# One decode step of attention and a bilinear GLU: scores moved to TensorE, P @ V moved to VectorE

## The chip, the cores and the metric

The kernel runs on one NeuronCore of a Trainium2 chip. The metric is the device time of one execution in microseconds (us); lower is better. The core has TensorE (PE in the profile; its weight loads are listed apart as PEld), VectorE (DVE), ScalarE (ACT), GpSimd (POOL) and SyncE (SP), and 16 DMA engines that share every large transfer.

## The reference, cut to what matters

```python
def _A_ref(x, k_cache, v_cache, wq, wo):          # B=2, D=448, H=16, Sk=8192, Dh=256, all f32
    q = (x @ wq).reshape(B, 1, H, Dh).transpose(0, 2, 1, 3)
    scores = jnp.einsum("bhqd,bhkd->bhqk", q, k_cache) * Dh ** -0.5
    p = softmax(scores, axis=-1)
    o = jnp.einsum("bhqk,bhkd->bhqd", p, v_cache)
    return o.transpose(0, 2, 1, 3).reshape(B, 1, H * Dh) @ wo

def _B_ref(x, w_gate, w_up, w_down):              # F=1792
    return ((x @ w_gate) * (x @ w_up)) @ w_down

h  = x + _A_ref(layernorm(x), ...)
h2 = h + _B_ref(layernorm(h), ...)
```

There are two batch rows with one query each. Every one of the 32 pairs of batch row and head reads its own 8 MB of K and 8 MB of V once; the caches are 537 MB of the 561 MB that the kernel reads.

## The kernel before, in words

The program is unrolled; nothing in it branches. It walks through 32 pairs (h, b), head by head, batch row 0 and then 1. Four tiles of 4 MB (32 KB in each of 128 partitions) form a ring with the tag `ring`. Each pair loads K into two of them and then V into the other two (`load_cache`, L146); a partition holds 32 whole keys of 256 numbers. SyncE issues all large loads in the order K, K, V, V, and waits before each until the ring tile that it overwrites has been read for the last time. Before the V loads of every fourth pair stands the load of the next weight tile `w`, which holds wq and wo of two heads (`load_w`, L140, 1792 KB).

Scores are made on VectorE. For each of the 64 keys of a partition, one SCALAR_TENSOR_TENSOR (L203) multiplies 256 numbers of K by the query, which stands in every partition, and its accumulator leaves the sum in a column of `s`. The accumulator is read out by an instruction of its own, DVE_READ_ACCUMULATOR, so a pair takes 128 VectorE instructions for its scores. The maximum over all keys goes DVE (L212), PE (L214), DVE (L216), PE (L218), ACT (L220), and one activation makes `p` (128 x 64, L223).

P @ V runs on TensorE (L234): 32 matmuls with two columns of `p` as the weights and two keys of V (512 numbers) as the moving operand, in four groups of PE columns. Then `o_ps` is copied (L239), transposed (L243), scaled (L249), and after batch row 1 multiplied by wo into `acc_ps` (2 x 448, L252).

After the last pair come the loads of the second half, on the same ring and queue: `wg_t`, `wu_t` (3136 KB each, L262) and `wd_t` in four parts (L271). The residual `h_sb` (L277) is transposed to `T_h`, centred and spread into `xr`; `g_ps` and `u_ps` (L299) are the two projections, `hm` (L323) their product, `hm_ps` and `hmT` its transpose, `y_ps` (L333) the output of w_down. Four small copies and one DMA (L346) write the result. A scheduler orders the instructions that lie between two loads.

Of the kernel before, what the change touches and what calls it, by code (L numbers as in the profile page):

```python
# [8 lines left out]
F32 = mybir.dt.float32  # L9
AF = mybir.ActivationFunctionType  # L10
# [5 lines left out]
P = 128  # L16
HALF = 64
DC = 4
DW = (P, P, P, HALF)
JC = 32  # L20
NCH = SK // (P * JC)
NJ = SK // P
RING = 4
WQ, WO = 3 * 2 * DH + DH, 4 * D
# [3 lines left out]
NF = F // P  # L28

# [8 lines left out]
def tile_decode_block(  # L38
# [3 lines left out]
    k_cache: bass.AP,  # L42
    v_cache: bass.AP,
# [10 lines left out]

# [6 lines left out]
    qpool = ctx.enter_context(tc.tile_pool(name="qpool", bufs=4))  # L61
    work = ctx.enter_context(tc.tile_pool(name="work", bufs=2))
    ps_q = ctx.enter_context(tc.tile_pool(name="ps_q", bufs=2, space=bass.MemoryType.PSUM))
    ps_s = ctx.enter_context(tc.tile_pool(name="ps_s", bufs=2, space=bass.MemoryType.PSUM))
    ps_1 = ctx.enter_context(tc.tile_pool(name="ps_1", bufs=1, space=bass.MemoryType.PSUM))


    x_sb = const.tile([B, DC * P], F32, name="x_sb")
    nc.scalar.dma_start(x_sb[:, :D], x.rearrange("b s d -> (b s) d"))
    nc.scalar.dma_start(x_sb[:, D:], x.rearrange("b s d -> (b s) d")[:, D - HALF :])  # L70
    ident = const.tile([P, P], F32, name="ident")
    make_identity(nc, ident)
    ones = const.tile([P, P], F32, name="ones")
    nc.vector.memset(ones, 1.0)
    avg = const.tile([P, P], F32, name="avg")
    nc.vector.memset(avg, 1.0 / D)
    row = const.tile([1, P], F32, name="row")
    nc.vector.memset(row, DH**-0.5)
    eps_t = const.tile([P, 1], F32, name="eps_t")
    nc.vector.memset(eps_t, EPS)  # L80
    xr = const.tile([P, DC + 1, B, 16], F32, name="xr")
    nc.gpsimd.memset(xr[:, DC - 1 :], 0.0)
    junk = [const.tile([P, DH], F32, name=f"junk{i}") for i in range(4)]

    sel = const.tile([P, 2], F32, name="sel")
    nc.vector.tensor_reduce(
        sel, ident.rearrange("p (g r) -> p r g", r=32)[:, :2, :], axis=AX.X, op=ALU.add
    )  # L90
    o_ps = [ps_1.tile([P, 2 * DH], F32, name=f"o_ps{i}") for i in range(2)]
    for t in o_ps:
        nc.vector.memset(t, 0.0)
    acc_ps = ps_1.tile([B, D], F32, name="acc_ps")
    y_ps = ps_1.tile([P, P], F32, name="y_ps")
# [12 lines left out]
    def center(h, tag):  # L108

        mean = ps_s.tile([P, B], F32, tag="sm", name=f"mean_{tag}")  # L110
# [10 lines left out]
    def spread(dst, src, n):  # L121

        for rows, c, to in LAYOUT:
            k = rows.stop - rows.start
            nc.vector.tensor_copy(
                dst[rows, to], src[rows, c][:, :, :, None].to_broadcast([k, c.stop - c.start, B, n])
            )

    def transposed(src, tag):
        ps = ps_s.tile([P, DC, B], F32, tag="sm", name=f"T_ps_{tag}")  # L130
        for c in range(DC):
            nc.tensor.transpose(ps[:, c, :], src[:, c * P : (c + 1) * P], ident[:B, :B])
        got = const.tile([P, DC, B], F32, name=f"T_{tag}")
        nc.vector.tensor_copy(got, ps)
        return got


    def load_w(hp):
        t = wpool.tile([P, WQ + WO], F32, tag="w", name=f"w_{hp}")
        nc.sync.dma_start(t, wqo[hp])  # L140
        return t

    def load_cache(src, b, h, c, name):
        t = ring.tile([P, JC, DH], F32, tag="ring", name=f"{name}_{h}_{b}_{c}")
        n = P * JC
        nc.sync.dma_start(t, src[b, h, c * n : (c + 1) * n].rearrange("(p j) d -> p j d", p=P))  # L146
        return t

    w_now = load_w(0)

    xT = transposed(x_sb, "x")


    xc = center(xT, "x")
    var = ps_s.tile([P, B], F32, tag="sm", name="var_x")
# [5 lines left out]
    xn = const.tile([P, DC, B], F32, name="xn")  # L161
    nc.vector.tensor_mul(xn, xc, rstd[:, None, :].to_broadcast([P, DC, B]))
    xb = const.tile([P, DC + 1, B, P], F32, name="xb")
    nc.gpsimd.memset(xb[:, DC - 1 :], 0.0)
    spread(xb, xn, P)

    def queries(hp, w):

        got = []
        for b in range(B):  # L170
            ps = ps_q.tile([P, 2 * DH], F32, tag="q", name=f"q_ps_{hp}_{b}")
            for c in range(DC - 1):
                nc.tensor.matmul(  # L173
                    ps, xb[:, c, b, :], w[:, c * 2 * DH : (c + 1) * 2 * DH],
                    start=(c == 0), stop=False,
                )
            for k in range(2):
                nc.tensor.matmul(  # L178
                    ps[:, k * DH : (k + 1) * DH], xb[:, DC - 1 + k, b, :],
                    w[:, 3 * 2 * DH : WQ], start=False, stop=(k == 1),  # L180
                )
            q = qpool.tile([P, 2, DH], F32, tag="q", name=f"q_{hp}_{b}")
            nc.scalar.activation(q.rearrange("p h d -> p (h d)"), ps, AF.Copy)  # L183
            got.append(q)
        return got
# [215 lines left out]
```

## Time and profile before

| | |
|---|---|
| runs | 1345.97, 1348.38, 1349.16 us; median 1348.38 us |
| profiled execution | span of 1345.7 us from the first to the last instruction; no other time of this execution is given, and the median of the runs lies 2.7 us above its span |
| PE busy | 496.5 us (37%), 2892 matmul records |
| DVE busy | 741.2 us (55%), 4232 instructions |
| ACT busy | 60.6 us (5%), 182 instructions |
| read from HBM | 561.19 MB, 417 GB/s over the span |
| DMA queue of the loads | its packets take 98.2% of the time of 16 DMA engines |
| mean granted TensorE clock | 0.656 |

Busy shares are means over the span. Where the profile lists windows, each row gives a stretch of time, the busy time of each engine in it with the number of instructions, the granted clock, the busy share of the 16 DMA engines and the GB/s that they moved. In the timeline, a row gives the start, the duration, the engine, the line and operation, the tiles written and read, and in brackets the idle time before it with what ended that. The queues q8 and q14 are marked `instruction`: they bring the program's own instructions to the engines.

### The profile page before, as it was taken

The page shows a single profiled execution, that of the slowest core. Times are in us where ns is not written, and L with a number is a line of the kernel's source. Part 1 is how long each engine was busy: PE and PEld are TensorE (multiplying, and loading weights), DVE is VectorE, ACT ScalarE, POOL GpSimd, SP SyncE. Part 2 cuts the span into 40 slices and gives each one's busy share as a digit, 9 for nine tenths or more (in the row PEclk, how much of TensorE's full clock was granted, in tenths as well). Part 3 has the DMA queues.
Part 4 walks back from the last instruction along what each step waited for, and adds up shares of the span by engine and source line. Part 5 has one row for each costly group of instructions (what it writes and reads, how often), then busy time and mean ns, then how long its engine had stood idle before and what let it go on. Part 6 is the DMA issues. An engine that isn't in the chain of part 4 may idle for free.

```text
span 1345.7 us, 10677 instructions
## 1 busy us (share of the span) xinstructions
PE 496.5 (37%) x2892; PEld 165.4 (12%) x2892; DVE 741.2 (55%) x4232; ACT 60.6 (5%) x182; POOL 1.2 (0%) x8
## 2 busy tenths in 40 slices
PE   3344223462224532155331533325343342333217
PEld 1111001120001210011100111101011020111003
DVE  5555664446654366653466634566444665445661
ACT  0000000000000000000000000000000000000000
POOL 0000000000000000000000000000000000000000
PEclk8667676675666865668655677656766576766569
DMA  9999999999999999999999999999999999999994
GB/s 405 428 433 430 433 429 430 431 430 433 432 426 433 430 432 432 428 433 430 425 412 417 430 433 408 411 411 430 430 407 412 413 435 426 411 407 414 417 404 189
DMA packets 20520, 561.87 MB, mean 418 GB/s; under 512 B 2280, under 2 KB 2412, under 8 KB 2668
## 3 DMA queue, kind: packets, MB, share of 16 engines
q1 hardware_dynamic: 20452, 561.20, 98.2%
q8 instruction: 22, 0.36, 0.1%
q14 instruction: 38, 0.31, 0.1%
q10 hardware_dynamic: 8, 0.00, 0.0%
HBM read 561.19 MB, written 0.00 MB: 417 GB/s over the span
## 4 chain that ended last, share of the span: by engine, by line
DMA 71%; DVE 27%; PE 1%; issue 1%; DVEq 0%; ACT 0%; SPq 0%
DMA k<-in_A_k_cache_dram 70%; DVE junk L203 27%; DMA wu_t<-in_B_w_up_dram 2%; PE u_ps L299 0%; PE y_ps L333 0%; DVE hm L323 0%; PE hm_ps L326 0%; DVEq L203 0%; DVE y L345 0%; ACT y L343 0%; SPq L140 0%; DVE hmT L328 0%; DVEq L323 0%
## 5 line engine op out<-in xcount | busy, mean ns | idle before, releaser
L203 DVE SCALAR_TENSOR_TENSOR junk<-k,q 128x256 f32<-128x256 f32 x2048 | 710.9, 420 | 483.6 <-DMA k<-in_A_k_cache_dram 483.6
L234 PE MATMUL o_ps<-v,p 128*2 128x512 f32 x2048 | 297.4, 741 | 37.2 <-DMA v<-in_A_v_cache_dram 37.0
L214 PE MATMUL mT<-ident,m 128*1 128x128 f32 x32 | 11.2, 351 | 624.0 <-DVE m L212 624.0
L203 DVE DVE_READ_ACCUMULATOR junk<-k,q 128x1 f32 x2048 | 168.2, 82 | 0.0
L173 PE MATMUL q_ps<-w,xb 128*128 128x512 f32 x96 | 60.7, 783 | 105.9 <-DMA w<-in_wqo_dram 104.5
L234 PEld LDWEIGHTS o_ps<-v,p 128*2 128x2 f32 x2048 | 53.5, 97 | 251.6 <-issue 197.7
L214 PEld LDWEIGHTS mT<-ident,m 128*1 128x1 f32 x32 | 2.6, 81 | 634.0 <-DVE m L212 613.5
L243 PE MATMUL oT_ps<-sel,o_sb 128*128 128x1 f32 x256 | 33.7, 253 | 23.2 <-ACT o_sb L239 23.2
L173 PEld LDWEIGHTS q_ps<-w,xb 128*128 128x128 f32 x96 | 23.6, 256 | 140.6 <-DMA w<-in_wqo_dram 114.7
L227 DVE RECIPROCAL rl<-l_ps 128x1 f32<-128x1 f32 x32 | 5.4, 169 | 62.9 <-PE l_ps L225 62.9
L252 PE MATMUL acc_ps<-w,oT 128*2 128x448 f32 x64 | 35.8, 695 | 5.6 <-ACT oT L249 5.6
L243 PEld LDWEIGHTS oT_ps<-sel,o_sb 128*128 128x128 f32 x256 | 31.0, 191 | 53.1 <-ACT o_sb L239 53.1
L220 ACT ACTIVATE nb<-nb_ps 128x1 f32<-128x1 f32 x32 | 5.5, 171 | 671.2 <-PE nb_ps L218 671.2
L239 ACT ACTIVATE o_sb<-o_ps 128x512 f32<-128x512 f32 x32 | 19.1, 597 | 353.7 <-PE o_ps L234 353.7
L225 PE MATMUL l_ps<-lsum,ones 128*128 128x1 f32 x64 | 17.3, 340 | 24.9 <-ACT p L223 24.9
L218 PE MATMUL nb_ps<-nm,row 1*128 1x1 f32 x64 | 16.7, 328 | 13.4 <-DVE nm L216 13.4
L216 DVE TENSOR_REDUCE nm<-mT 1x1 f32<-1x128 f32 x32 | 8.9, 279 | 20.4 <-PE mT L214 20.4
L183 ACT ACTIVATE q<-q_ps 128x512 f32<-128x512 f32 x16 | 9.6, 597 | 193.5 <-PE q_ps L178 193.5
L225 PEld LDWEIGHTS l_ps<-lsum,ones 128*128 128x128 f32 x64 | 14.6, 283 | 27.6 <-ACT p L223 27.6
L218 PEld LDWEIGHTS nb_ps<-nm,row 1*128 1x128 f32 x64 | 14.5, 280 | 23.1 <-issue 12.4
L178 PE MATMUL q_ps<-w,xb 128*128 128x256 f32 x64 | 16.5, 380 | 0.0
L178 PEld LDWEIGHTS q_ps<-w,xb 128*128 128x128 f32 x64 | 12.5, 195 | 9.5 <-issue 8.6
(74 smaller groups left out, 74.9 us busy)
## 6 DMA issues: line engine op xcount, KB each, us to landing
k<-in_A_k_cache_dram SPq DMA_DIRECT2D x64, 4096.0 KB, 28.6
v<-in_A_v_cache_dram SPq DMA_DIRECT2D x64, 4096.0 KB, 34.7
w<-in_wqo_dram SPq DMA_DIRECT2D x8, 1792.0 KB, 31.5
wg_t<-in_B_w_gate_dram SPq DMA_DIRECT2D x1, 3136.0 KB
wu_t<-in_B_w_up_dram SPq DMA_DIRECT2D x1, 3136.0 KB, 23.9
wd_t<-in_wd_dram SPq DMA_DIRECT2D x1, 1792.0 KB, 19.7
wd_t<-in_wd_dram SPq DMA_DIRECT2D x1, 672.0 KB, 21.0
wd_t<-in_wd_dram SPq DMA_DIRECT2D x1, 448.0 KB, 21.7
```

The lines of the kernel that those rows point to most:

```text
L173: nc.tensor.matmul(ps, xb[:, c, b, :], w[:, c * 2 * DH : (c + 1) * 2 * DH], start=(c == 0), stop=False,)
L178: nc.tensor.matmul(ps[:, k * DH : (k + 1) * DH], xb[:, DC - 1 + k, b, :], w[:, 3 * 2 * DH : WQ], start=False, stop=(k == 1),)
L183: nc.scalar.activation(q.rearrange("p h d -> p (h d)"), ps, AF.Copy)
L203: nc.vector.scalar_tensor_tensor(junk[j % 4], kt[c][:, j, :], 1.0, q_now[b][:, hh, :], op0=ALU.mult, op1=ALU.mult, accum_out=s[:, col : co ...
L214: nc.tensor.transpose(mT, m, ident)
L216: nc.vector.tensor_reduce(nm, mT, axis=AX.X, op=ALU.max, negate=True)
L218: nc.tensor.matmul(nb_ps, row, nm, start=True, stop=True)
L225: nc.tensor.matmul(l_ps, ones, lsum, start=True, stop=True)
L234: nc.tensor.matmul(o[g : g + 2, :], p[:, 2 * t : 2 * t + 2], vt[c][:, j : j + 2, :], start=(t < 4), stop=(t >= NJ // 2 - 4),)
L239: nc.scalar.activation(o_sb, o, AF.Copy)
L243: nc.tensor.matmul(oT_ps[:, c : c + 1], o_sb[:, (2 * k + c) * P : (2 * k + c + 1) * P], sel[:, k : k + 1], start=(k == 0), stop=(k == 1),)
L252: nc.tensor.matmul(acc_ps, oT[:, c, :], w_now[:, WQ + (hh * 2 + c) * D : WQ + (hh * 2 + c + 1) * D], start=(h == 0 and c == 0), stop=(h == ...
```

## The change: scores on TensorE, P @ V on VectorE, the output projection transposed, the last loads in parts

K is packed on the host so that the 256 numbers of a key lie over partitions (two blocks of 128), and the 8192 keys form 4 groups of 2048. A score matmul has a 128 x 32 weight, the query repeated in 32 columns, and 512 keys as the moving operand; four groups fill the four groups of PE columns. So `s` is a PSUM tile of 128 x 2048: 32 equal rows for each key group. V is packed so that a partition holds, for one key group, the 2048 keys of 8 of the 256 numbers. P @ V is then 8 VectorE instructions over 2048 keys, in place in the V tile, each with an accumulator. The packing is a change of layout; the loads of K and V keep their number, order and size (32 KB in each partition).

The query is made as columns (8 small matmuls in each head). `output` turns the sums into a 128 x 2 x 2 tile by four matmuls with `gsum` and multiplies by wo with wo as the weights: 10 matmuls in each head, with 2 columns moving, into a transposed `acc_ps`. It is called after the first half of the next pair's scores. The scheduler is switched off (`manual_schedule`). V of the last pair comes in four loads, `wu_t` in three, the result is written by two DMAs, and x arrives already transposed in one load.

```diff
+    ctx.enter_context(tc.manual_schedule())
...
+    def load_k(b, h):
+        got = []
+        for n in range(2):
+            t = ring.tile([P, 2, G, HK], F32, tag="ring", name=f"k_{h}_{b}_{n}")
+            nc.sync.dma_start(t.rearrange("p c g k -> p (c g k)"), kc[b, h, n])
...
+    xT = const.tile([P, DC, B], F32, name="xT")
+    nc.scalar.dma_start(xT.rearrange("p c b -> p (c b)"), x)
...
+    def scores(s, q, b, kt, n):
+        for j in range(HK // MM):
+            at = n * HK + j * MM
+            for c in range(2):
+                for g in range(G):
+                    nc.tensor.matmul(
+                        s[g * R : (g + 1) * R, at : at + MM],
+                        q[:, c, b, :],
+                        kt[n][:, c, g, j * MM : (j + 1) * MM],
+                        start=(c == 0), stop=(c == 1),
+                    )
+
+    def output(h, w, oacc, lsum):
+        l_ps = ps_m.tile([P, B], F32, tag="sm", name=f"l_ps_{h}")
+        nc.tensor.matmul(l_ps, ones, lsum, start=True, stop=True)
+        rl = work.tile([P, B], F32, tag="rl", name=f"rl_{h}")
+        nc.vector.reciprocal(rl, l_ps)
+        oT_ps = ps_m.tile([P, B, 2], F32, tag="sm", name=f"oT_ps_{h}")
+        for r in range(G):
+            nc.tensor.matmul(
+                oT_ps[r * R : (r + 1) * R], gsum, oacc[:, :, r::G], start=True, stop=True
+            )
+        oT = work.tile([P, B, 2], F32, tag="oT", name=f"oT_{h}")
+        nc.vector.tensor_mul(oT, oT_ps, rl[:, :, None].to_broadcast([P, B, 2]))
+        for m in range(DC + 1):
...
+            for c in range(2):
+                wo = w[:, h % 2, WQ + c * D : WQ + (c + 1) * D]
                 nc.tensor.matmul(
+                    acc_ps[rows, at, :], wo[:, at * P : at * P + rows.stop - rows.start],
+                    oT[:, :, c], start=(h == 0 and m == 0 and c == 0),
...
+    for i in range(NQ):
         h, b = divmod(i, B)
+        kt = load_k(b, h)
+        if h % 2 == 1 and b == 0 and h + 1 < H:
+            w_next = load_w((h + 1) // 2)
+        vt = load_v(b, h, 2 if i == NQ - 1 else 1)
...
-        for c in range(NCH):
-            for j in range(JC):
-                col = c * JC + j
-                nc.vector.scalar_tensor_tensor(
-                    junk[j % 4], kt[c][:, j, :], 1.0, q_now[b][:, hh, :],
-                    op0=ALU.mult, op1=ALU.mult, accum_out=s[:, col : col + 1],
-                )
+        s = ps_s.tile([P, GK], F32, tag="s", name=f"s_{i}")
+        scores(s, q_now, b, kt, 0)
+        if last is not None:
+            output(*last)
+            last = None
+        scores(s, q_now, b, kt, 1)
...
+        for n in range(2):
+            nc.vector.tensor_reduce(
+                m[:, n : n + 1], s[:, n * HK : (n + 1) * HK], axis=AX.X, op=ALU.max
+            )
...
+        p = work.tile([P, GK], F32, tag="p", name=f"p_{i}")
+        nc.scalar.activation(p, s, AF.Exp, bias=nb, scale=1.0, accum_out=lsum[:, b : b + 1])
...
-        for t in range(NJ // 2):
-            c, j = divmod(2 * t, JC)
-            g = 32 * (t % 4)
-            nc.tensor.matmul(
-                o[g : g + 2, :], p[:, 2 * t : 2 * t + 2], vt[c][:, j : j + 2, :],
-                start=(t < 4), stop=(t >= NJ // 2 - 4),
+        for o in range(NO):
+            v = vt[o // (NO // 2)][:, o % (NO // 2), :]
+            nc.vector.scalar_tensor_tensor(
+                v, v, 1.0, p, op0=ALU.mult, op1=ALU.mult, accum_out=oacc[:, b, o : o + 1]
             )
...
+    wg_t = load_ff(wg, "wg_t", ())
+    wu_t = load_ff(wu, "wu_t", (2 * F, 3 * F))
+    wd_t = load_ff(wd, "wd_t", (8 * D, 11 * D, 13 * D))
...
+    output(*last)
+    hT = const.tile([P, DC, B], F32, name="hT")
+    nc.vector.tensor_add(hT, xT, acc_ps)
```

On VectorE, the end of the last pair and what follows it. In these rows `k_1_1` is the second K tile of batch row 1, `m` and `nm` the maximum, `rl` the reciprocal of the sum, `h_sb` the residual. Before, the last of the 64 score instructions stand in front of the maximum:

```order
L203 SCALAR_TENSOR_TENSOR junk_99,s_4369<-k_1_1_4363,q_1_3775 128x256
L203 SCALAR_TENSOR_TENSOR junk_100,s_4369<-k_1_1_4363,q_1_3775 128x256
L212 TENSOR_REDUCE m_4434<-s_4369 128x1
L216 TENSOR_REDUCE nm_4438<-mT_4436 1x1
L227 RECIPROCAL rl_4449<-l_ps_4447 128x1
L277 TENSOR_TENSOR h_sb<-x_sb,acc_ps 2x448
L278 TENSOR_TENSOR h_sb<-x_sb,acc_ps 2x64
L134 COPY T_h<-T_ps_h 128x8
L100 TENSOR_REDUCE sum_h_h<-T_h 128x2
```

Now, with `oacc` for the sums over a V tile and `ff_ps` for the PSUM tile of the second half:

```order
L241 TENSOR_REDUCE m_2657<-s_2623 128x1 x2
L247 TENSOR_REDUCE nm_2662<-mT_2656 1x1
L263 SCALAR_TENSOR_TENSOR v_1_0_2617,oacc_2535<-v_1_0_2617,p_2668 128x2048 x4
L263 SCALAR_TENSOR_TENSOR v_1_1_2620,oacc_2535<-v_1_1_2620,p_2668 128x2048 x4
L286 MEMSET ff_ps 64x128 x2
L287 MEMSET ff_ps 128x112
L197 RECIPROCAL rl_2695<-l_ps_2693 128x2
L204 TENSOR_TENSOR oT_2702<-oT_ps_2697,rl_2695 128x4
L291 TENSOR_TENSOR hT<-xT,acc_ps 128x8
L120 TENSOR_REDUCE sum_h_h<-hT 128x2
```

The long VectorE work moved from in front of the maximum, where it needs K, to behind it, where it needs V and `p`; it is 8 instructions a pair where 64 stood.

On TensorE, the last pair up to the first projection. Before, with `o_ps` for P @ V:

```order
L214 MATMUL mT_4436<-ident,m_4434 1x128
L218 MATMUL nb_ps_4440<-nm_4438,row 128x1
L225 MATMUL l_ps_4447<-lsum_4445,ones 128x1
L234 MATMUL o_ps_104<-v_1_0_4365,p_4444 2x512 x16
L234 MATMUL o_ps_104<-v_1_1_4367,p_4444 2x512 x16
L243 MATMUL oT_ps_4485<-sel,o_sb_4483 128x1 x4
L252 MATMUL acc_ps<-w_3690,oT_4359 2x448 x2
L132 MATMUL T_ps_h<-ident,h_sb 128x2 x4
```

Now, with `s` for the scores:

```order
L185 MATMUL s_2623<-k_1_0_2613,q_2517 32x512 x16
L185 MATMUL s_2623<-k_1_1_2615,q_2517 32x512 x16
L245 MATMUL mT_2656<-ident,m_2657 1x128 x2
L251 MATMUL nb_ps_2664<-nm_2662,row 128x1
L195 MATMUL l_ps_2693<-lsum_2536,ones 128x2
L200 MATMUL oT_ps_2697<-oacc_2535,gsum 32x4 x4
L210 MATMUL acc_ps<-oT_2702,w_2209 128x2 x6
L210 MATMUL acc_ps<-oT_2702,w_2209 64x2 x4
L130 MATMUL mean_h<-sum_h_h,avg 128x2
```

The 32 large matmuls moved from behind the maximum to in front of it. Behind the last V load stand now four small matmuls and ten with wo as their weights, where the second half of P @ V, its transpose and two matmuls stood.

More of the change, by code (lines that the diff above doesn't have):

```diff
@@ L92, in tile_decode_block @@
[L92 to L95, printed above, removed]
+    acc_ps = ps_1.tile([P, DC, B], F32, name="acc_ps")
     def over_chunks(t, tag):
@@ L160, in tile_decode_block @@
     nc.vector.reciprocal(rstd, std)
[L161 to L172, printed above, removed]
+    xn = const.tile([P, DC + 1, B], F32, name="xn")
@@ L285, in tile_decode_block, with project @@
     )
[L287 to L290 removed]
+    def project(ps, w):
         for c in range(DC):
```

314 lines of the change are left out of this document (160 added, 154 removed).

## The prediction, made before the changed kernel ran

> **What bounds the kernel now.** I read the page first, from engines to DMA.
>
> ```profile
> span 1345.7 us, 10677 instructions
> PE 496.5 (37%) x2892; PEld 165.4 (12%) x2892; DVE 741.2 (55%) x4232; ACT 60.6 (5%) x182; POOL 1.2 (0%) x8
> ...
> GB/s 405 428 433 430 433 429 430 431 430 433 432 426 433 430 432 432 428 433 430 425 412 417 430 433 408 411 411 430 430 407 412 413 435 426 411 407 414 417 404 189
> ...
> q1 hardware_dynamic: 20452, 561.20, 98.2%
> q8 instruction: 22, 0.36, 0.1%
> q14 instruction: 38, 0.31, 0.1%
> ...
> k<-in_A_k_cache_dram SPq DMA_DIRECT2D x64, 4096.0 KB, 28.6
> v<-in_A_v_cache_dram SPq DMA_DIRECT2D x64, 4096.0 KB, 34.7
> w<-in_wqo_dram SPq DMA_DIRECT2D x8, 1792.0 KB, 31.5
> ```
>
> No engine is over 55% busy, while the loads keep 16 DMA engines busy 98.2% of the time. The bytes stay as they are, so at first sight neither does the time move. The next view asks how fast the loads run in each stretch (columns: window, us, busy us of each engine, clock, DMA share, GB/s):
>
> ```profile
> 60.00:350.00 290.00, 108.12 (x595) 35.23 (x595) 163.41 (x936) 12.69 (x39) 0.00 (x0) 0.65 1.00 431
> 350.00:640.00 290.00, 106.55 (x591) 35.05 (x591) 161.95 (x928) 12.69 (x39) 0.00 (x0) 0.65 1.00 431
> 660.00:960.00 300.00, 115.65 (x659) 37.64 (x651) 160.22 (x917) 13.54 (x41) 0.00 (x0) 0.67 0.99 421
> 960.00:1300.00 340.00, 112.78 (x652) 35.09 (x652) 196.06 (x1123) 12.96 (x42) 0.00 (x0) 0.62 0.99 417
> 1328.00:1341.00 13.00, 10.26 (x147) 5.21 (x149) 2.56 (x12) 0.69 (x1) 0.00 (x0) 1.00 0.07 27
> ```
>
> The last row is the key: for the last 13 us of loading, 0.07 of the DMA engines work at 27 GB/s, a sixteenth of 431. **One DMA engine is 13 us late**, 15 have finished, and a load has landed only when all 16 have done their part. In the first half all run at 431 GB/s; from 660 us on the mean falls, because a ring tile can't be loaded again before the late engine has filled it, and the 15 wait.
>
> When did it fall behind? The chain of waits shows how far apart K lands (start, us: the K load ends at their sum):
>
> ```profile
> 480.06 28.55 DMA k<-in_A_k_cache_dram
> 519.88 28.54 DMA k<-in_A_k_cache_dram
> 559.70 28.57 DMA k<-in_A_k_cache_dram
> ```
>
> A pair takes 39.82 us, twice alike. Its 16.78 MB at 431 GB/s are 38.93 us. So the late engine loses 0.9 us in every pair. The DMA view of 60 to 640 us (14.5 pairs) says what else it may carry:
>
> ```profile
> q8 instruction: 9, 0.15, 0.1%
> q14 instruction: 17, 0.14, 0.1%
> ```
>
> These bring instructions. On the page, q8 moved 16 KB a fetch, 0.36 MB in all, 62 bytes for each of PE's 5784 records; q14 8 KB a fetch. At 62 bytes, 8 KB are some 130 instructions, and VectorE executes 4232/32 = 132 in a pair: one fetch of q14 in each pair (17 in 14.5 pairs, the rest for ACT, POOL or SP), which is the rhythm of the loss. q8 comes every 64 us and can't make equal pairs. I conclude: VectorE's fetches all go through one DMA engine, and each costs it 0.9 us (itself, and what it disturbs). 33 fetches make 30 us. The other side agrees: 13 us of lateness at the end, and the 15 engines' waiting, 300 x (1 - 421/431) + 340 x (1 - 417/431) = 18 us: 31 us.
>
> **How late V is.** The loads up to the last V are 128 x 4.194 + 8 x 1.835 = 551.5 MB, 1279.7 us at 431 GB/s. The first is issued by 1.13 us; I take 1.5 for its start:
>
> ```profile
> 0.74 0.39 SPq L140 DMA_DIRECT2D w<-in_wqo_dram  x1
> ```
>
> So the last V could land at 1281 us. The tail of the timeline shows that it lands at 1318.4:
>
> ```profile
> 1309.63 0.22 DVE L212 TENSOR_REDUCE m<-s 128x1 f32<-128x64 f32 x1
> ...
> 1311.53 0.35 ACT L223 ACTIVATE p<-s,nb 128x64 f32<-128x64 f32 x1
> ...
> 1312.54 5.46 PE L234 MATMUL o_ps<-v,p 128*2 128x512 f32 x32
> ...
> 1318.38 3.62 PE L234 MATMUL o_ps<-v,p 128*2 128x512 f32 x32 [0.39 <-DMA v<-in_A_v_cache_dram]
> ...
> 1322.71 1.05 PE L243 MATMUL oT_ps<-sel,o_sb 128*128 128x1 f32 x8 [0.72 <-ACT o_sb L239]
> ...
> 1324.12 1.67 PE L252 MATMUL acc_ps<-w,oT 128*2 128x448 f32 x4 [0.35 <-ACT oT L249]
> ...
> 1326.93 0.17 DVE L134 COPY T_h<-T_ps_h 128x8 f32<-128x8 f32 x1 [0.37 <-PE T_ps_h L132]
> ...
> 1328.56 3.63 PE L299 MATMUL g_ps<-wg_t,xr 128*32 128x512 f32 x32 [0.50 <-DVE xr L125]
> ...
> 1333.56 3.63 PE L299 MATMUL u_ps<-wu_t,xr 128*32 128x512 f32 x32 [1.06 <-DMA wu_t<-in_B_w_up_dram]
> ...
> 1339.03 3.23 PE L333 MATMUL y_ps<-wd_t,hmT 128*2 128x128 f32 x112 [0.28 <-DVE hmT L328]
> ...
> 1342.33 0.28 DVE L345 COPY y<-y_ps 2x128 f32<-2x128 f32 x1 [3.36 <-PE y_ps L333]
> ...
> 1343.51 0.32 SPq L346 DMA_DIRECT2D out_dram<-y  x1
> ```
>
> It is 37 us late, 30 of them by VectorE's fetches; 7 remain, for TensorE's fetches and what I can't name. Behind it lies a tail of 1345.7 - 1318.4 = 27.3 us.
>
> **The change, part by part.** *Fetches.* VectorE's program falls from 4232 instructions to about 676: 420 in the new order, and 256 accumulator reads, one for each of the long instructions. That is 5.3 fetches, 4.8 us instead of 30. TensorE's grows: 1593 matmuls of two records each (but the 68 transposes), each with a weight load, are 6236 records against 5784, so 24 fetches of q8 instead of 22. If they spread over the DMA engines, each engine gets one or two; a 16 KB fetch at 27 GB/s is 0.6 us, with the same disturbance (0.9 less the 0.3 us of 8 KB) 1.2: 2 us for an engine. Loss after: 7 us. Bounds: 5 (VectorE's alone) and 12 (all 7 of the unnamed remain). The last V lands at 1.5 + 1279.7 + 7 = 1288 us, **30 us earlier**.
>
> A page of the Trainium skill speaks against this: Runtime: NRT & Kernel Launch, Instruction fetch mechanics, says that instructions are refilled in 16 KiB blocks by a DMA queue of the sequencer's own and that crossing a block is mostly hidden. By it fewer instructions would save nothing, and the time would be the first rival's. The trace agrees for the waiting instruction, and q8's blocks have that size; q14's are half as large, and what the page leaves out is the load whose DMA engine fetches.
>
> *Does the stream stay fed?* Prices first:
>
> ```profile
> 1308.82 0.42 DVE L203 SCALAR_TENSOR_TENSOR junk<-k,q 128x256 f32<-128x256 f32 x1
> ...
> 1309.17 0.42 DVE L203 SCALAR_TENSOR_TENSOR junk<-k,q 128x256 f32<-128x256 f32 x1
> ```
> ```profile
> L239 ACT ACTIVATE o_sb<-o_ps 128x512 f32<-128x512 f32 x32 | 19.1, 597 | 353.7 <-PE o_ps L234 353.7
> L225 PEld LDWEIGHTS l_ps<-lsum,ones 128*128 128x128 f32 x64 | 14.6, 283 | 27.6 <-ACT p L223 27.6
> L220 ACT ACTIVATE nb<-nb_ps 128x1 f32<-128x1 f32 x32 | 5.5, 171 | 671.2 <-PE nb_ps L218 671.2
> L323 DVE TENSOR_TENSOR hm<-u_ps,g_sb 128x512 f32<-128x512 f32 x1 | 0.7, 692 | 4.4 <-PE u_ps L299 4.4
> ```
>
> VectorE starts a 256-wide instruction every 0.35 us. L323 with 512 elements takes 692 - 420 = 272 ns more than one with 256: 1.06 ns an element, so a 2048-wide one takes 0.35 + 1.90 = 2.25 us (at most 8 x 0.35 = 2.8). Eight are 18.0 us, where 64 took 22.1. A score half is 16 matmuls of 512 columns in four groups, the form of L234: 5.5 us after a pause, 3.6 behind other work. Counted from the landing of the second K tile: scores 5.5, maximum over 1024 from PSUM 1.2 (692 ns and 512 more elements), the small steps 1.9 (from 1309.85 to 1311.53 before, and a transpose more), exponential 2.1 (0.83 ns a column by L239 and L220, 2048 columns, and the accumulator). VectorE starts P @ V at 10.7, when the first V tile (9.7) is there, and ends at 28.7. The V tiles are free at 19.7 and 28.7; their next loads begin at four and five loads after K's landing, 39 and 49. K is free 5 us after landing, needed 29 after. So the queue keeps 20 us in hand everywhere. PE's `output` stands between two score halves and waits for VectorE's 28.7; the K tile of the half in front of it lands at 29: nothing waits. In VectorE's order `rl` waits for that PE step, with an idle VectorE behind it. The start (x in one load of tiny pieces, on ACT's queue; fewer query columns) hides behind 43 us of loads issued at once: the first K tile must be free by 43, and was at 29.
>
> ```profile
> 29.07 28.14 DMA k<-in_A_k_cache_dram
> ...
> 1318.06 1.81 SPq L271 DMA_DIRECT2D wd_t<-in_wd_dram  x4
> ```
>
> The start costs nothing unless x is 14 us late. The four extra issues (two for V, two for wu) take SP 0.45 us each by the second row, within its 20 us; I put them at nothing, and at 2 us if that cover were gone.
>
> *The tail, from the last V landing.* VectorE ends its 8 instructions at 28.7 - 19.5 = 9.2 us; halves of V don't help, since VectorE is behind anyway. Then oT_ps 0.9 (1.05 before, with wider weights) and its product 0.2; ten matmuls with wo as weights, 12 loads of 128 columns at 14.6/64 = 0.23 and 8 of half the width: 3.8; `hT` 0.3; from there to g_ps 1.5 as from T_h before: g_ps starts at 15.9, where it was 10.2. It no longer waits 1.1 us for wu behind g_ps, but seven residual matmuls moved there (0.7): u_ps at 20.6 instead of 15.2. From there to y_ps as before, 5.5 and 3.2; one copy instead of four saves 0.9. PE comes to this from 18 us of rest, and its first 16 matmuls may take 5.5 instead of 3.6: I add 0.7, bounds 0 and 2. Tail: 27.3 + 5.4 - 0.9 + 0.7 = 32.5 us, **5 us longer** (bounds 30 and 35). The loads of the second half ended 22.6 us behind V (1341), and y_ps begins at 26 behind it: they are covered.
>
> **Sum.** 1288 + 32.5 = 1320.5 us of span. The median of the runs, 1348.38, is 2.7 us above the profiled span; so 1323 us, 1.9% faster.
>
> **The rivals.** *The late engine stays late* (the slower side): its 0.9 us a pair come from somewhere else, a fixed slowness. Then the last V lands at 1318.4 as before, and the longer tail decides: 1318.4 + 32.5 = 1350.9, with 2.7 us 1354. It decides as soon as the stream gains less than 5 us. For it: I infer which queue does it from the rhythm. Against it: 132 instructions a pair fit one block too well. The Trainium skill knows such a case, DMA: Bandwidth & Descriptors, Latency and other measured facts: DMA engines 7 and 15 are usually slower, which it ascribes, unsure, to descriptor rings of the GpSimd path. Here one engine is late, not two, and no queue of that path carries loads.
>
> *Both fetch queues on the late engine.* Then of 30 us, 22 fetches of q8 have the larger part, by bytes 0.36 MB to 33 x 8 KB = 0.27 MB: 17 us; 24 of them cost 19, VectorE's 5 some 2. The stream gains 9, the tail takes 5: 1342, median 1345, about no change. Against it: the two pairs above are alike although q8 comes only every 64 us.
>
> *A new stall takes part of the gain*: a ring tile that is released late, or one DMA engine that gets three or four of TensorE's fetches. Each us of it is one; 8 to 15 us give 1331 to 1338.
>
> **How the numbers follow.** The forecast has 0.80. Its upper end is 1331: loss 12 and tail 35. Its lower end is 1313: loss 5, tail 30, and a stream at the 433 GB/s of the better slices, since 431 still contains the late engine (551.5 MB take 6 us less). The new stall has 0.09, both queues 0.05, the fixed slowness 0.06. The range 1313 to 1336 takes in the greater part of the new stall and leaves out some 0.15. A change of 0.3%, 4 us, is about what this measurement can tell from none. Faster: 0.89 (the forecast and the new stall), within 0.3%: 0.05, slower: 0.06.
>
> **What would show it.** q14 with about 10 fetches instead of 38 (some six come ahead of the start); 430 GB/s in all windows up to the end of V; no stretch in which a sixteenth of the DMA engines works alone for 13 us; pairs 38.9 to 39.1 us apart; the last V near 1288. For the tail: VectorE's last long instruction 9 us behind the last V, acc_ps about 4 us long, and an end that no DMA decides. If the fetches fall and the pairs still take 39.8 us, my reading of the late engine is wrong.

## The result, and the profile after

The changed kernel takes 1324.25 us (median of 4 runs, 1323.21 to 1324.97) where the kernel before, run beside it, took 1347.18 us: a ratio of 0.983 (95% interval 0.9816 to 0.9844). The profiled execution has a span of 1323.2 us and took 1324.97 us.

From the page of the kernel after, the span, the engines, the GB/s of each slice and the DMA queues:

```profile
span 1323.2 us, 7506 instructions
PE 499.9 (38%) x3114; PEld 200.2 (15%) x3114; DVE 669.7 (51%) x674; ACT 79.3 (6%) x116; POOL 0.8 (0%) x8
...
GB/s 401 428 436 426 435 430 431 427 435 430 428 433 429 433 430 431 428 432 430 432 432 429 432 430 429 429 433 429 429 433 432 429 431 431 429 428 434 433 422 214
...
q1 hardware_dynamic: 21032, 561.20, 98.8%
q8 instruction: 24, 0.39, 0.1%
q14 instruction: 9, 0.07, 0.0%
```

VectorE executes 674 instructions where it executed 4232, and q14 brings 9 blocks instead of 38. TensorE's q8 brings 24 instead of 22. The GB/s row no longer sinks to 404 to 417 in its second half. The windows say the same (us of PE, PEld, DVE, ACT and POOL, then granted clock, DMA share, GB/s; the last two rows are the end of the loads):

```profile
60.00:350.00 290.00, 114.23 (x692) 46.17 (x688) 145.38 (x141) 16.71 (x25) 0.00 (x0) 0.63 1.00 431
...
660.00:960.00 300.00, 121.77 (x709) 45.15 (x709) 148.85 (x145) 16.43 (x24) 0.00 (x0) 0.62 1.00 431
960.00:1260.00 300.00, 107.04 (x671) 44.30 (x675) 164.16 (x159) 18.94 (x28) 0.00 (x0) 0.63 1.00 431
1304.00:1309.50 5.50, 5.50 (x32) 1.85 (x24) 0.39 (x2) 0.00 (x0) 0.00 (x0) 0.54 0.55 222
1309.50:1320.00 10.50, 7.97 (x166) 4.99 (x164) 1.27 (x5) 0.69 (x1) 0.00 (x0) 1.00 0.01 5
```

The DMA engines are full to the end of the walk over the pairs. In the last 5.5 us of loading they still work at half their rate, 0.55 and 222 GB/s, so none of them is left alone for long. The stretch of 13 us with a sixteenth of the bandwidth is gone, and the last load lands 32 us earlier, at 1309.5 instead of 1341. In the chain of waits, K lands at the sums of these rows (start and duration):

```profile
475.11 34.21 DMA k<-in_kc_dram
...
514.77 33.45 DMA k<-in_kc_dram
...
553.48 33.96 DMA k<-in_kc_dram
```

That is 509.32, 548.22 and 587.44: pairs 38.9 and 39.2 us apart, where they were 39.82. The tail of the timeline (start, us, engine, line and operation, tiles; in brackets the idle time before it and what ended that):

```profile
1268.10 5.33 PE L185 MATMUL s<-k,q 128*32 128x512 f32 x32 [4.60 <-DMA k<-in_kc_dram]
...
1273.51 2.35 DVE L241 TENSOR_REDUCE m<-s 128x1 f32<-128x1024 f32 x2 [15.93 <-PE s L185]
...
1277.31 1.97 ACT L255 ACTIVATE p<-s,nb 128x2048 f32<-128x2048 f32 x1
...
1279.40 2.29 DVE L263 SCALAR_TENSOR_TENSOR v<-v,p 128x2048 f32<-128x2048 f32 x1 [2.76 <-ACT p L255]
...
1294.89 2.29 DVE L263 SCALAR_TENSOR_TENSOR v<-v,p 128x2048 f32<-128x2048 f32 x1
...
1298.34 3.25 PE L210 MATMUL acc_ps<-oT,w 128*128 128x2 f32 x20 [0.84 <-DVE oT L204]
...
1303.35 6.47 PE L312 MATMUL ff_ps<-wg_t,xr 128*32 128x512 f32 x32 [0.50 <-DVE xr L295]
...
1311.36 0.40 PE L333 MATMUL ff_ps<-ident,hT 128*2 128x112 f32 x14 [1.23 <-ACT g_sb L326]
1311.55 3.63 PE L312 MATMUL ff_ps<-wu_t,xr 128*32 128x512 f32 x32
...
1317.00 2.87 PE L351 MATMUL ff_ps<-wd_t,hmT 128*2 128x112 f32 x112 [0.28 <-DVE hmT L346]
...
1320.24 1.09 ACTq L361 DMA_DIRECT2D out_dram<-y  x1
```

The last half of the scores starts when K lands, at 1268.10. The maximum, the exponential and eight VectorE instructions follow, and then the small steps up to the output. Two rows are longer than I had thought: the first projection on `wg_t` takes 6.47 us (L312), and the residual matmuls (L333) wait 1.23 us for an ACT instruction.

### The profile page after: what moved, and what is told of

Read it like the earlier page. It is cut to its first block, busy times and chain, and to the rows that moved or that the text cites. A ratio compares the mean times of both kernels' runs of the same rounds, so it can differ in the third digit from the quotient of the medians.

```text
span 1323.2 us, 7506 instructions
## 1 busy us (share of the span) xinstructions
PE 499.9 (38%) x3114; PEld 200.2 (15%) x3114; DVE 669.7 (51%) x674; ACT 79.3 (6%) x116; POOL 0.8 (0%) x8
## 4 chain that ended last, share of the span: by engine, by line
DMA 83%; PE 15%; DVE 2%; issue 0%; ACT 0%; SPq 0%; DVEq 0%; ACTq 0%
DMA k<-in_kc_dram 83%; PE s L185 13%; DVE v L263 1%; PE ff_ps L312 1%; PE acc_ps L210 0%; PE ff_ps L351 0%; DVE m L241 0%; ACT p L255 0%; DVE hm L342 0%; ACT g_sb L326 0%; PE ff_ps L344 0%; PE mean_h L130 0%; DVE nm L247 0%; SPq L80 0%; PE ff_ps L333 0%
## 5 line engine op out<-in xcount | busy, mean ns | idle before, releaser
L263 DVE SCALAR_TENSOR_TENSOR v<-v,p 128x2048 f32<-128x2048 f32 x256 | 569.5, 2287 | 120.1 <-ACT p L255 70.6
L185 PE MATMUL s<-k,q 128*32 128x512 f32 x2048 | 360.7, 869 | 693.8 <-DMA k<-in_kc_dram 693.8
L241 DVE TENSOR_REDUCE m<-s 128x1 f32<-128x1024 f32 x64 | 75.4, 1219 | 403.8 <-PE s L185 403.8
L185 PEld LDWEIGHTS s<-k,q 128*32 128x32 f32 x2048 | 87.0, 152 | 925.9 <-issue 822.6
L255 ACT ACTIVATE p<-s,nb 128x2048 f32<-128x2048 f32 x32 | 62.9, 1967 | 1.2 <-ACT nb L253 0.2
L165 PE MATMUL q_ps<-xn,w 128*128 128x2 f32 x192 | 40.2, 325 | 0.8 <-PE var_x L142 0.8
L165 PEld LDWEIGHTS q_ps<-xn,w 128*128 128x128 f32 x192 | 38.2, 290 | 1.1 <-PE var_x L142 0.9
L210 PE MATMUL acc_ps<-oT,w 128*128 128x2 f32 (+1 forms) x320 | 31.1, 239 | 6.3 <-DVE oT L204 6.3
L210 PEld LDWEIGHTS acc_ps<-oT,w 128*128 128x128 f32 (+1 forms) x320 | 29.5, 179 | 7.9 <-DVE oT L204 7.7
L263 DVE DVE_READ_ACCUMULATOR v<-v,p 128x1 f32 x256 | 20.9, 82 | 0.0
L168 PE MATMUL q_ps<-xn,w 128*128 128x2 f32 x64 | 16.7, 330 | 0.0
L168 PEld LDWEIGHTS q_ps<-xn,w 128*128 128x128 f32 x64 | 15.8, 302 | 0.0
## 6 DMA issues: line engine op xcount, KB each, us to landing
wu_t<-in_B_w_up_dram SPq DMA_DIRECT2D x1, 896.0 KB, 27.9
```

Of the source, the lines that this page charges most:

```text
L165: nc.tensor.matmul(ps[:, c, :], wh[:, at : at + P], xn[:, k, :], start=(k == 0), stop=False)
L168: nc.tensor.matmul(ps[:, c, :], wh[:, 3 * DH : WQ], xn[:, DC - 1 + c, :], start=False, stop=True)
L185: nc.tensor.matmul(s[g * R : (g + 1) * R, at : at + MM], q[:, c, b, :], kt[n][:, c, g, j * MM : (j + 1) * MM], start=(c == 0), stop=(c == 1),)
L210: nc.tensor.matmul(acc_ps[rows, at, :], wo[:, at * P : at * P + rows.stop - rows.start], oT[:, :, c], start=(h == 0 and m == 0 and c == 0) ...
L241: nc.vector.tensor_reduce(m[:, n : n + 1], s[:, n * HK : (n + 1) * HK], axis=AX.X, op=ALU.max)
L255: nc.scalar.activation(p, s, AF.Exp, bias=nb, scale=1.0, accum_out=lsum[:, b : b + 1])
```

## The experiments

My theory: the stream of loads was late because one DMA engine also fetched VectorE's program, and the change won by shortening that program. Rivals: the new order of the loads or the new layout won it; or that engine is simply slow; or the fetches of any engine cost as much.

### The instructions put back

On the kernel after, nothing is changed but for small instructions that do nothing useful: 112 one-column memsets on VectorE in each of 31 pairs, or 56, or 112 on GpSimd, or 28 small matmuls on TensorE.

```diff
+    fill = const.tile([P, 4], F32, name="fill")
...
+        if i < NQ - 1:
+            for z in range(112):
+                nc.vector.memset(fill[:, z % 4 : z % 4 + 1], 0.0)
```

112 on VectorE. Expected:

> The changed kernel with 112 one-column memsets on VectorE in each of 31 pairs, put where VectorE waits for the scores. They take some 7 us of a pair in which VectorE is idle for about 18 us, so they add instructions to fetch (3472 x 62 bytes = 215 KB, 27 blocks of 8 KB) and next to no time of their own. Fetch theory (one DMA engine carries all of VectorE's fetches and loses 0.9 to 1.0 us by each): 24 to 27 us slower, 1348 to 1351 us, and at the end one DMA engine works alone for some 13 us again. Order theory (the gain came from the new layout, the order of the instructions or the earlier release of the K tiles): no change, 1324 us. Slow-engine theory (one DMA engine is slow whatever it fetches): no change either.

56 on VectorE. Expected:

> The same with 56 memsets in a pair: 1736 instructions, 13.6 blocks. Fetch theory: 12 to 13.5 us slower, 1336 to 1338 us, half of the step with 112. Order theory and slow-engine theory: 1324 us. A theory by which VectorE's time and not its fetches counts would give a threshold: nothing here, something with 112.

112 on GpSimd. Expected:

> The 112 memsets in a pair are on GpSimd, which has no other work, instead of VectorE. If each engine's fetches have a DMA engine of their own, as I suppose for the queue q14, GpSimd's 27 blocks make another DMA engine late by 24 to 27 us: 1348 to 1351 us. If q14 spreads fetches of engines other than VectorE, or if it is VectorE's execution that costs: 1324 to 1326 us.

28 on TensorE, without the tile `fill`. Expected:

> 28 one-column f32 matmuls in a pair on TensorE, behind the exponential: 112 records (two matmuls and two weight loads each), 3472 in all as before, 13.6 blocks of 16 KB on queue q8. If q8 spreads its fetches over the 16 DMA engines: 1 to 2 us slower, 1325 to 1326 us. If q8 uses one DMA engine as VectorE's fetches do: 13.6 x 1.2 to 1.6 = 16 to 22 us slower, 1340 to 1346 us.

All four ran beside a kernel before of 1347.74 us. From the page, q14 and one window at the end of the loads of the run with 112 on VectorE, then q14 and the first window with 56, the same with 112 on GpSimd, and q8 with the matmuls:

```profile
q14 instruction: 36, 0.29, 0.1%
...
1320.00:1325.00 5.00, 4.02 (x24) 1.84 (x28) 1.70 (x11) 0.00 (x0) 0.00 (x0) 0.50 0.07 29
```
```profile
q14 instruction: 22, 0.18, 0.0%
...
60.00:350.00 290.00, 109.31 (x685) 44.31 (x681) 157.57 (x541) 16.72 (x25) 0.00 (x0) 0.64 1.00 433
```
```profile
q14 instruction: 36, 0.29, 0.1%
...
60.00:350.00 290.00, 107.64 (x630) 42.48 (x630) 142.60 (x138) 16.60 (x25) 83.28 (x2119) 0.62 1.00 429
```
```profile
q8 instruction: 38, 0.62, 0.2%
```

| | us | ratio to before (95%) | fetches more than after |
|---|---|---|---|
| 112 on VectorE | 1342.75 | 0.9963 (0.9950 to 0.9976) | 27 of q14 |
| 56 on VectorE | 1328.62 | 0.9861 (0.9846 to 0.9876) | 13 of q14 |
| 112 on GpSimd | 1331.72 | 0.9878 (0.9861 to 0.9895) | 27 of q14 |
| 28 on TensorE | 1327.66 | 0.9851 (0.9836 to 0.9866) | 14 of q8 |

The direction is right. With the 27 fetches back, the stretch in which a sixteenth of the DMA engines works alone is back too (0.07, 29 GB/s). But all three q14 runs are faster than the fetch theory said: by 5 us or more with 112, by 7 or more with 56, and by 16 or more with GpSimd if its fetches cost as much as VectorE's. The TensorE run is 1.7 us above the range for fetches that spread. Their windows gave the hint: the run with 56 streamed at 433 GB/s in its first window (above), the kernel after at 431 in the same one. What the three share and the TensorE run lacks is the tile `fill`. It takes 16 bytes a partition, and the ring tiles behind it move from byte 25056 to byte 25088 of a partition. So a control was needed that has the tile and nothing else:

```diff
+    fill = const.tile([P, 4], F32, name="fill")
+    nc.vector.memset(fill, 0.0)
```

> The kernel after, with one more tile of 16 bytes a partition (one memset at the start), which moves the ring tiles from byte 25056 of a partition to byte 25088, from a multiple of 32 to a multiple of 512. It is in the three runs that added work on VectorE or GpSimd, which all streamed at 433 GB/s where the kernel after has 431. If the place of the destination sets the speed: windows of 433 GB/s, 0.44% of 1280 us or 5 to 6 us less, 1318 to 1320 us. If the added instructions themselves did it, or the chip's day: 1324 us and 431 GB/s.

It takes 1318.97 us (ratio 0.9792, 0.9777 to 0.9807): 5.3 us less than the kernel after, for 32 bytes. Two of its windows:

```profile
60.00:350.00 290.00, 109.90 (x696) 45.28 (x692) 145.49 (x141) 16.72 (x25) 0.00 (x0) 0.65 1.00 433
...
660.00:960.00 300.00, 110.60 (x720) 41.64 (x712) 149.17 (x145) 18.62 (x28) 0.00 (x0) 0.65 1.00 433
```

This is the base for the three runs. Against it, 27 fetches of VectorE cost 23.8 us, or 0.88 each, and 13 cost 9.7, or 0.74. Between the two lie 14 fetches and 14.1 us: 1.0 us each. On GpSimd the same number of fetches cost 12.8 us, 0.47 each. GpSimd waits for nobody and ran ahead: 2119 of its 3472 memsets lie between 60 and 350 us, and the row after 350 us has none. The 14 fetches of q8 cost 3.4 us, 0.24 each, though their blocks are twice as large. So TensorE's fetches don't gather on one engine.

The trace's records of single packets show more. They name no DMA engine, but during the loads nearly every packet starts within 16 ns of the end of another, so the packets fall into 16 chains, one for each engine. (Where two packets end at the same moment, one chain can be taken for another.) In the run with 56 memsets, 19 of the 22 fetches of q14 lie in one chain; the other three, which the control has within 10 us of the same times, lie elsewhere. That chain ends its last load at 1314.9 us, the 15 others between 1301.2 and 1303.6. In the control, six fetches of q14 lie in one chain, and those of q8 go round over eight others. GpSimd's 27 lie in one chain too.

The chains also give the price of a fetch to its engine. Each of q14 takes 0.31 us, and the next 32 KB packet behind it takes 1.75 us instead of 1.21 where VectorE's block was fetched (control and 56 memsets), 1.56 where it was GpSimd's: 0.84 and 0.65 us together. What the kernel loses is less, because in the control the chains end between 1298.5 and 1303.6 us, VectorE's at 1302.8, and lateness up to the last of them is hidden. That lowers the price of the first 13. For GpSimd, an estimate from these numbers is 1298.5 + 27 x 0.65 = 1316.1 us, if its engine carries no other fetches; in that run one chain ends at 1316.7 us and the others by 1306.9.

### The instructions taken out of the kernel before

This is the test from the other side: order, layout, engines and loads are those of the kernel before (its ring stands at a multiple of 32 bytes, not of 64, like that of the kernel after), and only the number of score instructions falls. Each of them then leaves one sum over 8 or 2 keys, so these two kernels no longer have a score for every key.

```diff
+        nc.vector.memset(s, 0.0)
         for c in range(NCH):
-            for j in range(JC):
+            for j in range(0, JC, 8):
...
-                    junk[j % 4], kt[c][:, j, :], 1.0, q_now[b][:, hh, :],
+                    junk[j // 8 % 2].rearrange("p (j d) -> p j d", d=DH),
+                    kt[c][:, j : j + 8, :], 1.0,
+                    q_now[b][:, hh, None, :].to_broadcast([P, 8, DH]),
```

> The kernel before, order and engines as they were, but each score instruction of VectorE takes 8 keys at once (2048 elements, one sum over the 8 keys, so the scores are not the reference's; one memset of s a pair). VectorE has 21 instructions a pair instead of 132, some 690 in all. If VectorE's fetches make the one DMA engine late: some 28 fetches fewer at 0.95 us, q14 near 10, no stretch at the end with one engine alone, 1318 to 1322 us. If the lateness is a fixed slowness of that engine, or belongs to the old layout or order of the loads: about 1347 us. The ring tiles stand at a multiple of 32 bytes as before, so the stream's speed is 431 GB/s.

> The same with 2 keys (512 elements) in each score instruction, a sum over both: 69 VectorE instructions a pair, some 2200 in all. By the fetches: 15 to 16 fewer at 0.95 us, q14 near 22, about 1332 us, half way. If only the number of large instructions or VectorE's busy time counted, which hardly moves here, 1345 to 1348 us.

With 8 keys an instruction it takes 1317.08 us (ratio 0.9776, 0.9759 to 0.9793), with 2 keys 1327.53 us (0.9852, 0.9835 to 0.9868). With 8 keys, q14, a late window, and the moment when the last V lands:

```profile
q14 instruction: 10, 0.08, 0.0%
...
960.00:1260.00 300.00, 111.83 (x651) 34.56 (x651) 134.04 (x147) 12.96 (x42) 0.00 (x0) 0.66 1.00 431
...
1286.31 3.61 PE L237 MATMUL o_ps<-v,p 128*2 128x512 f32 x32 [1.69 <-DMA v<-in_A_v_cache_dram]
```

With 2 keys:

```profile
q14 instruction: 22, 0.18, 0.0%
...
60.00:350.00 290.00, 110.48 (x595) 36.01 (x595) 150.51 (x501) 12.69 (x39) 0.00 (x0) 0.68 1.00 431
```

Without any other part of the change, 28 fetches fewer make the kernel before 30.4 us faster, 1.08 us each. The last V lands at 1286.31 instead of 1318.38, and the windows stand at 431 GB/s. With 16 fewer it is 19.9 us. The rivals of order, layout and a slow DMA engine expected 1345 to 1348 us for both and fall. So does VectorE's busy time as the cause: with 2 keys it falls only from 163.4 to 150.5 us in the window from 60 to 350 us (second row above), and two thirds of the gain are there.

With 8 keys it is also 7 us faster than the kernel after, at the same 431 GB/s. The difference is the tail: its span of 1314.2 us ends 27.9 us behind the last V, about as before (27.3). P @ V behind the maximum on VectorE was no gain by itself; the count of instructions was.

### The tail

Two waits are taken away first. In the last pair, the maximum of the first half is issued before the second half of the scores, and `g_ps` gets a PSUM bank of its own.

```diff
         scores(s, q_now, b, kt, 0)
+        if i == NQ - 1:
+            nc.vector.tensor_reduce(m[:, 0:1], s[:, :HK], axis=AX.X, op=ALU.max)
...
-    g_ps, u_ps, y_ps = ff[:, 0], ff[:, 1], ff[:, 3, :OC]
+    g_ps = ps_1.tile([P, MM], F32, name="g_ps")
+    u_ps, y_ps = ff[:, 1], ff[:, 3, :OC]
```

> Tail of the kernel after, two false waits taken away: the first half's maximum of the last pair is issued ahead of the second half's scores, and g_ps gets a PSUM bank of its own, so that the residual matmuls don't wait for its copy to g_sb. If these waits are on the path: the first maximum ends before the second half's scores and 2.3 us go from the row of the two maxima, and the residual matmuls start at once behind var instead of 1.2 us later; 2 to 3 us less behind the last K, 1321 to 1322 us. If the scores' second half now waits for the first maximum, or another wait takes their place: 1324 us.

1321.2 us (ratio 0.9808, 0.9793 to 0.9823), 3 us less. In its timeline, the second maximum, `g_ps`, and the residual matmuls behind `var_h`:

```profile
1273.62 1.23 DVE L242 TENSOR_REDUCE m<-s 128x1 f32<-128x1024 f32 x1 [8.75 <-PE s L185]
...
1302.21 5.32 PE L315 MATMUL g_ps<-wg_t,xr 128*32 128x512 f32 x32 [0.50 <-DVE xr L298]
...
1307.46 0.38 PE L323 MATMUL var_h<-avg,sr 128*128 128x1 f32 x2
1307.77 0.39 PE L336 MATMUL ff_ps<-ident,hT 128*2 128x112 f32 x14
```

One reduction stands on the path where two stood, and the residual matmuls start as `var_h` ends. Both waits were false: the parts of a tile that were written and read had nothing to do with each other, but the wait was for the tile. `g_ps` itself is 1.15 us shorter, which I hadn't expected. Its new tile isn't the reason: in the next run it lies in `ff_ps` again and takes 5.09 us. The trace's records of the granted clock explain it. The clock is either 0.50 or 1.00 and changes only on steps that are 3.41 us apart, and in all 14 traces `g_ps` takes 3.63 us and half of the time for which the clock is 0.50 in it, within 0.05 us. That time was 5.76 us in the kernel after and 3.45 us here. So of the 3.6 us between the two profiled spans (1323.2 and 1319.6), 1.15 came from where `g_ps` fell on these steps, and not from a wait.

Next, TensorE is kept at work during the last P @ V, by matmuls whose result nobody reads.

```diff
+            if i == NQ - 1 and o < NO - 1:
+                nc.tensor.matmul(spare[:, :1], ident, oacc[:, b, o : o + 1], start=True, stop=True)
+                for z in range(3 if o < NO - 2 else 2):
+                    nc.tensor.matmul(spare, ident, p[:, :MM], start=True, stop=True)
```

> The kernel after with TensorE kept at work while VectorE does the last P @ V: behind each of its first seven instructions one matmul that reads that sum and two or three of 512 columns into an unused PSUM bank (27 more matmuls). If g_ps at 6.47 us is long because TensorE rested for 19 us and its granted clock is about 0.5: g_ps 3.6 us, acc_ps 1.9 instead of 3.25, and 3 to 4 us less in all, 1320 to 1321 us. If the length of g_ps comes from wg_t or from the memsets of its tile: g_ps stays near 6.5 and the time 1324.

It takes 1327.22 us, 3 us more (ratio 0.9853, 0.9838 to 0.9868). First two windows of the kernel after, over `acc_ps` and `g_ps`; then, of the run with fillers, the windows over the fillers, `acc_ps` and `g_ps`; then from its timeline VectorE's last long instruction, one group of fillers, `l_ps` and `acc_ps`:

```profile
1298.30:1301.70 3.40, 3.25 (x20) 3.15 (x20) 0.05 (x1) 0.00 (x0) 0.00 (x0) 0.50 1.01 420
1303.30:1309.70 6.40, 6.35 (x32) 2.05 (x32) 0.97 (x6) 0.00 (x0) 0.00 (x0) 0.55 0.60 243
```
```profile
1288.00:1303.80 15.80, 15.80 (x47) 7.72 (x46) 10.88 (x13) 0.00 (x0) 0.00 (x0) 1.00 1.00 419
1304.60:1306.50 1.90, 1.84 (x20) 1.73 (x20) 0.00 (x0) 0.00 (x0) 0.00 (x0) 1.00 0.57 234
1308.00:1313.00 5.00, 4.96 (x32) 1.78 (x32) 0.96 (x6) 0.00 (x0) 0.00 (x0) 0.70 0.15 52
```
```profile
1296.10 2.29 DVE L265 SCALAR_TENSOR_TENSOR v<-v,p 128x2048 f32<-128x2048 f32 x1
...
1299.25 2.82 PE L273 MATMUL spare<-p,ident 128*128 128x512 f32 x6
...
1303.85 0.28 PE L195 MATMUL l_ps<-lsum,ones 128*128 128x2 f32 x2
...
1304.65 1.84 PE L210 MATMUL acc_ps<-oT,w 128*128 128x2 f32 x20 [0.35 <-DVE oT L204]
```

The cause was right and the remedy wrong. In the kernel after, TensorE runs `acc_ps` at a granted clock of 0.50 and `g_ps` at 0.55. Behind the fillers it runs `acc_ps` at 1.00, in 1.84 us instead of 3.25, and `g_ps` at 0.70, in 5.09 instead of 6.47. But three fillers take 2.82 us and VectorE's step 2.21, 0.94 us for each of them where 16 score matmuls of 512 columns took 5.33 (above), 0.33 each even at a low clock: those run four side by side in groups of 32 columns, and my price was theirs. VectorE is done at 1298.4, and TensorE comes to `l_ps`, which stands behind the fillers, at 1303.85.

All of it together, with the same number of fillers:

> The kernel after with all of it: the 16-byte tile, the early maximum, g_ps in a bank of its own (which takes the filler matmuls first), and the filler matmuls. If the parts add up: 1324 less 5.5, 2.5 and 3.5, or 1312 to 1313 us. If the end is set by the loads of the second half once the tail is shorter (they land 13.5 us ahead of the end), the gain stops short of that; I don't expect it.

1320.53 us (0.9803, 0.9788 to 0.9819), a miss of 8 us for the same reason. Then without fillers, and with fewer of them:

> The 16-byte tile, the early maximum and g_ps in a bank of its own, without fillers. If the gains measured apart (1324.25 to 1318.97, and to 1321.2) add up: 1316 us. If the shorter stream only makes the tail wait, it stays at 1318 to 1319 us.

> All tail changes and the 16-byte tile as before, but fewer filler matmuls: two of 512 columns behind each of the first five VectorE instructions, one behind the next two (12 instead of 20). In the run with 20 a filler took 0.86 us of TensorE, twice my price, three of them 2.8 us against VectorE's 2.21, and the output step came 5.7 us late. With two, 2.0 us fit into 2.21: the output step comes on time, acc_ps takes 1.84 and g_ps about 5.1 us; against the version without fillers 1.5 to 2.5 us less, 1313 to 1315 us. If the fillers run at half clock, they need 3.6 us a step and end late again: 1316 to 1319 us.

Without fillers 1315.89 us (0.9769, 0.9749 to 0.9788; 1315.51 to 1317.08): the tile's place and the two waits add up. With 12 fillers 1314.57 us (0.9754, 0.9734 to 0.9773; 1313.49 to 1315.08), 1.3 us less than without, where I expected 1.5 to 2.5. In its timeline the output step now comes on time, 0.14 us behind the start of VectorE's last accumulator readout:

```profile
1290.02 0.08 DVE L269 DVE_READ_ACCUMULATOR v<-v,p 128x1 f32 x1
1290.16 0.23 PE L202 MATMUL oT_ps<-oacc,gsum 128*32 128x4 f32 x2 [0.32 <-DVE v L269]
...
1291.14 1.84 PE L212 MATMUL acc_ps<-oT,w 128*128 128x2 f32 x20 [0.75 <-DVE oT L206]
...
1294.53 5.01 PE L325 MATMUL g_ps<-wg_t,xr 128*32 128x512 f32 x32 [0.50 <-DVE xr L308]
```

This is the fastest version that ran, 10 us below the kernel after and 32 us below the kernel before.

## Why the prediction was right, and where it was not

**One DMA engine is late.** Right. The last load lands 32 us earlier, and no stretch is left in which one engine works alone.

**VectorE's fetches are the cause, 0.9 us each.** Right. The two tests from opposite sides gave 0.74 to 1.24 us each: 0.74 for the first 13 put back, 1.0 for the next 14, 0.87 for the step from 10 fetches to 22 in the kernel before, 1.24 for the step from 22 to 38. Why the last step cost more than the others isn't settled. That q14 serves the same DMA engine every time was inferred in the prediction; the packet records show it. In the kernel before, the 14 fetches from 406 to 928 us lie in one chain, from 489 us on the one furthest behind, and each takes 0.9 to 1.0 us of it: 0.31 to 0.33 itself, the rest by the next packet. Of the Trainium skill's section on instruction fetch (Runtime: NRT & Kernel Launch, Instruction fetch mechanics) the part holds that says a crossing is mostly hidden, for the engine that executes: in the kernel before, the score instructions of a pair start 0.34 to 0.35 us apart with one exception of 0.42. For the loads beside it, 28 crossings cost 30 us here.

**TensorE's fetches spread.** Right in kind: 14 more cost 0.24 us each. They go round over eight engines and not sixteen, VectorE's not among them in the control, and one takes some 1.5 us of its engine and not 1.2 (1.0 to 1.1 itself and 0.5 by the next packet, in the run with the small matmuls). The prediction added 2 us for TensorE to VectorE's 4.8 as if they met on one engine. The second rival, both queues on one engine, falls with that.

**How late V is.** VectorE is behind V anyway, so no row shows its landing. The second half of the last scores shows that of K: 1268.10, where the prediction's 1288 - 19.5 gives 1268.5. By that, 6.6 of the 7 us of loss that I took are there. The kernel before with 8 keys shows V itself at 1286.31, a loss of 5 us, the lower bound.

**From K to the output step.** P @ V starts 11.3 us behind K instead of 10.7 and ends 29.1 behind it instead of 28.7. The exponential was priced well (2.0 for 2.1), and so was the long VectorE instruction (2.21 us apart for 2.25). The maximum was not: I took one reduction of 1.2 us, and both wait for the whole of `s` (2.35). `acc_ps` took 3.25 for 3.8. So `g_ps` starts at 1303.35, where the prediction has 1303.9.

**The first projection.** This is the term that was mis-sized. I added 0.7 us for a TensorE that comes from rest, with 2 as the bound; it was 6.47 - 3.63 = 2.8 us. The rows say why: a granted clock of 0.50 for the first 5.76 us of `g_ps`, and 1.00 behind that.

```profile
1303.35:1309.11 5.76, 5.76 (x30) 2.05 (x32) 0.92 (x6) 0.00 (x0) 0.00 (x0) 0.50 0.63 258
1309.11:1309.80 0.69, 0.69 (x5) 0.06 (x1) 0.00 (x0) 0.00 (x0) 0.00 (x0) 1.00 0.22 83
```

I had read the price of the rest from one row of the kernel before, 5.46 us against 3.62, and took a third of it. The Trainium skill's TensorE: Matmul & The Clock Gate, Part 1: The HAM clock gate, says that a rested TensorE runs at half its clock until it has been busy for about 3.4 us; `acc_ps` at 0.50 for 3.25 us agrees. By that rule `g_ps` would take an estimated 5.3 us if its busy time counts from its own start (3.4 at half the clock do 1.7 us of its work, and 1.9 remain). Here the rise came 2.35 us later than that, because it comes on a step of 3.41 us and `g_ps` had started between two of them; in the run with the two waits taken away it started 0.04 us ahead of one, and took 5.32.

**The residual matmuls.** The prediction put them in place of a wait of 1.1 us for wu. A wait of 1.23 us for `g_sb` came with them, because both write the one tile `ff_ps`. With the two together the tail ends at 1323.2 instead of 1320.5, 2.7 us late.

**The sum.** The run of the profile lies 1.8 us above its span, not 2.7, and the median 1324.25 lies 1 us above the span. So 2.7 us too little in the tail met 1.7 us too much between span and median, and 1323 came within 1.3 us of the median. That closeness is luck; the span itself was predicted 2.7 us too short. The edits that I costed at nothing cost nothing that shows: x in one load of small pieces, four more issues on SP, `output` between two score halves. The third rival, a new stall, did not come: the DMA share is 1.00 in every window up to 1260 us.

## What to carry to other kernels

When all loads slow down together and the end of the profile shows a stretch with a sixteenth of the bandwidth, look for what else one DMA engine carries; the number of instructions on VectorE is a cost to the loads even where VectorE is idle for half of the time. What the rewrite won came from fewer and wider instructions alone, since they won as much on the old order; so count instructions before an algorithm is moved between engines, and count what the move does to the tail. In the tail behind the last load, look at granted clock and at waits for a tile of which another part is meant.

## What the runs showed of the hardware that was not expected

A shift of the destination by 32 bytes changed the speed of all loads. With the ring tiles at byte 25056 of a partition the windows read 431 GB/s, at byte 25088 they read 432 to 433, and the kernel is 5.3 us faster. In the trace's records of single packets, nearly all 32 KB packets take 1213 ns in the second case, and 1214 to 1224 ns in the first. 25056 is a multiple of 32, 25088 of 512; which power of two in between matters wasn't tried.

GpSimd's program comes through q14 as well (36 blocks with its 3472 memsets against 9). Its 27 more blocks all took time from one DMA engine, 0.65 us each where VectorE's took 0.84, and the kernel lost 12.8 us.

A fetch costs the DMA engine more than its own packet: in the kernel before, 0.31 to 0.33 us for the 8 KB, and up to 0.66 us more for the 32 KB packet that follows it.

The granted clock of TensorE changes only on steps of 3.41 us. The same projection of 32 matmuls took 5.01 to 6.60 us where the clock was 0.50 for a part of it, by where it began on these steps, and 3.63 us in the kernel before, where it was 1.00 throughout.
